# Twelve late attention slots as 64 tokens of two batches, in quarters and eighths of TensorE's array

## The chip, the cores and the metric

One core of a Trainium2 chip runs the kernel. The metric is device time in microseconds (us) of one execution; lower is better. TensorE (PE) multiplies, VectorE (DVE), ScalarE (ACT) and GpSimd (POOL) do elementwise work, SyncE (SP) issues most transfers. PEld is TensorE's loading of weights, which runs beside its matmuls. PSUM, which takes the results of matmuls, has 8 banks of 512 fp32 values for each of 128 partitions.

## The reference

A linear attention with a decaying state, whose output goes through a layer with a cosine gate. Only the shapes and the formulas that matter:

```
r, k, v: (4 batches, 8 heads, 768 tokens, 48), w, u: (8 heads, 48), fp32
for t in range(S):
    cur = einsum('bhd,bhe->bhde', u * k[t], v[t])
    y[t] = einsum('bhd,bhde->bhe', r[t], state + cur)
    state = w * state + einsum('bhd,bhe->bhde', k[t], v[t])
x = y.transpose(0, 2, 1, 3).reshape(3072, 384)
h = x @ w_in            # (384, 2048), float64 weights
out = (h * cos(h)) @ w_out   # (2048, 384), float64 weights; out is (3072, 384)
```

## The kernel before, in words

**Attention.** The recurrence is done in chunks of 128 tokens. There are 24 slots, one for each chunk of each batch (6 chunks, 4 batches): slot i is batch i % 4, chunk i // 4. In a slot, k and r are turned so that the head dimension lies on partitions (kT, rT: 4 pairs of heads, two heads on partitions 0 to 47 and 64 to 111) and scaled by powers of w (decT_k, decT_r). Then

- the scores: 8 matmuls, one a head, 48 rows by 128 columns, into two banks (mm_a, L819). The two heads of a pair lie in different row halves of the array;
- the diagonal with the bonus u (ACT, L809) and the mask, which copies the scores above the diagonal into it (DVE, L826): the result is A;
- x, the slot's output: a carried part from the state (mm_x, L840: 12 matmuls of 112 rows by 32 columns, four side by side in the array) and a direct part from A and v (mm_x2, L853: 16 matmuls of 128 rows by 32 columns), accumulated in one bank and split by ACT and DVE into two reduced-precision parts, xh and xl;
- the state of this batch: 8 matmuls of 128 rows by 48 columns (mm_z, L875), added to zc and decayed by DVE (L932, L933). The last chunk of a batch needs none.

All of these matmuls are fp32, and the profile shows two records for each.

**The layer.** Eight blocks of three slots (384 tokens). For each block and each of 16 slices f of the hidden dimension there is a step: nine matmuls into h (mm_h, L316), a chain of six operations between ACT and DVE for the gate (L327, L330, L333, L1030, L1033, L1036), and nine matmuls into the output (mm_o, L322). The first four blocks go through the slices in four pieces (UNITS), while the weights are being converted; the other four go through all 16 slices one after the other. Outputs of the first four blocks are added up in memory by transfers that POOL issues (L1078); those of the others are stored once, by SP (L1076), the very last by ACT (L1074).

**Late slots.** The first 12 slots (XS) run at the start. Slots 12 to 23 are late: each runs beside the steps of a block before its own, its matmuls set between those of the steps, in two groups: the scores, and later x with the state (mm_xz). Instead of transposing k and r with TensorE, SP loads them in rows of four tokens into a raw buffer (load_s, L693: four transfers a buffer, 32 partitions each), and DVE (L738) and POOL (L743) turn and scale them. The raw buffers (R_raw, two) are shared with the loads of the weights (L506, L511), which come a second time for a check of their range (L521, L532). PSUM banks 5 to 7 (B_ATT) serve the late slots.

**Order.** Every operation is an Op with an engine, a due time, an assumed cost, and what it comes after. A planner (Plan.order) lays them out by a greedy list, sixty times with changed due times, keeps the best by its own replay and fixes the order of each engine. The hardware then waits only where data or buffers ask for it.

Of the kernel before, what the change touches and what calls it, by code (L numbers as in the profile page):

```python
# [33 lines left out]
XS = 12  # L34
# [20 lines left out]
class Tile:  # L55
    def __init__(self, ap):
        self.ap, self.owner = ap, None

# [16 lines left out]
class Plan:  # L75
# [18 lines left out]
    @staticmethod  # L94
    def _free_at(tile):

        if tile.owner is None:
            return 0.0
        if any(o.end is None for o in tile.owner.users):
            return None  # L100
        return max(o.end + o.lat for o in tile.owner.users)

    def _ready(self, o):
        t = max((d.end + d.lat for d in o.after), default=0.0)
        picks, taken = [], set()
        for b in o.bufs:
            if b.tile is not None:
                continue
            best = None
            for tl in b.tiles:  # L110
                if id(tl) in taken:
# [6 lines left out]
            taken.add(id(best[1]))  # L118
            picks.append((b, best[1]))
            t = max(t, best[0])  # L120
        return t, picks

    def latest(self, order):
# [3 lines left out]
        for o in order:  # L127
# [8 lines left out]
            for b in o.bufs:  # L136
                owners = tiles.setdefault(b.tile, [])
                if not owners or owners[-1][0] is not b:
                    if all(b is not x for x, _ in owners):
                        owners.append((b, o))  # L140
# [10 lines left out]
    def replay(self, order, rng):  # L151

        free, port, prev, owner, end = {}, 0.0, {}, {}, {}
        for o in order:
            t = max((end[d] + d.lat for d in o.after), default=0.0)
            for b in o.bufs:
                if owner.get(b.tile) is not b:
                    prev[b] = owner.get(b.tile)
                    owner[b.tile] = b
                if prev.get(b) is not None:  # L160
                    t = max(t, max(end[d] + d.lat for d in prev[b].users))
# [35 lines left out]
    def one_pass(self):  # L197
        for o in self.ops:
            o.start = o.end = None
            for b in o.bufs:  # L200
                b.tile = None
                for tl in b.tiles:
                    tl.owner = None
# [13 lines left out]
        while len(done) < len(self.ops):  # L217
# [16 lines left out]
            for b, tl in picks:  # L234
                b.tile, tl.owner = tl, b
# [15 lines left out]
def kernel(  # L251
# [18 lines left out]
    C = 128  # L270
    NP = H // 2
# [5 lines left out]
    NJ = B * CPB  # L277
    TB = max(BLOCKS) * C
# [57 lines left out]
    with ExitStack() as actx:  # L336
# [3 lines left out]
        bank = [Tile(banks.tile([P, 512], F32, name=f"bank{i}")) for i in range(8)]  # L340
# [26 lines left out]

        zc = [att.tile([KP, NP, D], F32, name=f"zc{b}") for b in range(B)]
        R_zt = ring("zt", 2, [KP, NP, 2 * D], F32)
        wr = att.tile([NP, 2, DP], F32, name="wr")  # L370
# [8 lines left out]
        dec_k = att.tile([P, H, D], F32, name="dec_k")  # L379
        upper = att.tile([P, C], I32, name="upper")  # L380
        warm = att.tile([P, P], BF16, name="warm")
# [20 lines left out]
        def start_pool2():  # L402
            for t in R_zt:
                nc.gpsimd.memset(t.ap, 0.0)
# [11 lines left out]

        def start_dve():
# [5 lines left out]
        o_pool2 = op(POOL, -98, 3.0, start_pool2)  # L423
        o_dve = op(DVE, -99, 0.3, start_dve)
# [54 lines left out]
        o_dk = op(ACT, -6, 0.45, tab_copy, [o_tt], [b_tab])  # L479

# [175 lines left out]
        def chunk(i, due, xbuf):  # L656
            b, c = i % B, i // B
# [21 lines left out]
            late = i >= XS  # L679
            if late:  # L680
                rb = Buf(R_f)
                ks, rs = Buf(R_raw), Buf(R_raw)

            def rn():
                return heads(rb) if late else rb()[:, :, 0:D]
# [4 lines left out]
            def load_s(buf, src):  # L690
                def part(m, q, n_q, p, n_p, n):
                    j, d0 = m // 2, 32 * (m % 2)
                    nc.sync.dma_start(  # L693
                        staged(buf)[32 * m + q : 32 * m + q + n_q, p : p + n_p, 0:n],
                        bass.AP(
                            tensor=src.tensor,
                            offset=src.offset + ((b * H + 2 * p + j) * S + c * C + 4 * q) * D + d0,
                            ap=[[4 * D, n_q], [2 * S * D, n_p], [1, n]],
                        ),
                    )  # L700

                def go():
                    for m in range(3):
                        part(m, 0, 32, 0, NP, 4 * D)
                    if i < NJ - 1:
                        part(3, 0, 32, 0, NP, 4 * D)
                    else:

                        nc.gpsimd.memset(staged(buf)[96:P, NP - 1, 4 * D - 32 :], 0.0)
                        part(3, 0, 32, 0, NP - 1, 4 * D)  # L710
                        part(3, 0, 31, NP - 1, 1, 4 * D)
                        part(3, 31, 1, NP - 1, 1, 4 * D - 32)

                return go


            ahead = [last_A[0]] if late else []
            ln = "late" if late else None
            if late:
                l_ks = op(SP, due - 6.2, 2.2, load_s(ks, k), ahead, [ks], lat=4.0, line=ln)  # L720
                l_rs = op(SP, due - 6.1, 2.2, load_s(rs, r), ahead, [rs], lat=4.0, line=ln)
            l_k = op(SP, due - 5.2, 1.2, load(kb, k), ahead, [kb], lat=2.6, line=ln)
            l_r = op(SP, due - 5.1, 1.2, load_r, ahead, [rb], lat=2.6, line=ln)
            l_v = op(SP, due - 5.0, 1.2, load(vb, v), ahead, [vb], lat=2.6, line=ln)
# [9 lines left out]
            if late:  # L734
                def tr_s(dst, src):
                    def go():
                        blocks = staged(src).rearrange("q p (g x) -> q p g x", g=4)[:, :, :, 0:32]
                        nc.vector.transpose(dst().rearrange("q p (t g) -> q p g t", g=4), blocks)  # L738

                    return go  # L740

                def decay_s(dst, dec):
                    return lambda: nc.gpsimd.tensor_tensor(dst()[0:KP], dst()[0:KP], dec[0:KP], op=ALU.mult)  # L743

                t_k = op(DVE, due - 2.9, 0.95, tr_s(kT, ks), [l_ks], [ks, kT])
                e_k = op(POOL, due - 2.8, 1.4, decay_s(kT, decT_k), [t_k], [kT], port=True)
                t_r = op(DVE, due - 2.8, 0.95, tr_s(rT, rs), [l_rs], [rs, rT])
                e_r = op(POOL, due - 2.7, 1.4, decay_s(rT, decT_r), [t_r], [rT], port=True)
            else:
                t_r = op(PE, due - 2.4, 0.49, tr(rTp, rb), [l_r, o_pool], [rb, rTp, rT], lat=0.3)  # L750
                e_r = op(
                    DVE,
                    due - 2.2,
                    0.62,
                    lambda: nc.vector.tensor_tensor(rT()[0:KP], cube(rTp)[0:KP], decT_r[0:KP], op=ALU.mult),
                    [t_r, o_dtr],
                    [rTp, rT],
                )
# [29 lines left out]
            if not first and not late:  # L788
# [32 lines left out]
            last_A[0] = o_A = op(PE, due - 1.7, 1.25 if late else 1.1, mm_a, [e_k, e_r], [kT, rT, *Ap], lat=0.3)  # L821
# [426 lines left out]
```

## Time and profile before

| what | value |
|---|---|
| three runs, median | 513.16 us (512.38 to 513.32) |
| profiled execution, time | 512.26 us |
| profiled execution, span (first to last instruction) | 510.5 us |
| granted TensorE clock, mean | 0.999 |
| TensorE busy | 501.5 us, 98% of the span |
| DVE, ACT, POOL busy | 381.0, 331.0, 177.1 us |

Rows of groups read: line, engine, operation, output<-inputs, shapes, count | busy us, mean ns of one | idle time before and who ended it. A row of the chain has a start, a length, and the work. A row of waits has who waited for whom: us in total, times, the longest. A row of a timeline has start, length, engine, line and operation.

### The profile page before, as it was taken

The page shows a single profiled execution, that of the slowest core. Times are in us where ns is not written, and L with a number is a line of the kernel's source. Part 1 is how long each engine was busy: PE and PEld are TensorE (multiplying, and loading weights), DVE is VectorE, ACT ScalarE, POOL GpSimd, SP SyncE. Part 2 cuts the span into 40 slices and gives each one's busy share as a digit, 9 for nine tenths or more (in the row PEclk, how much of TensorE's full clock was granted, in tenths as well). Part 3 has the DMA queues.
Part 4 walks back from the last instruction along what each step waited for, and adds up shares of the span by engine and source line. Part 5 has one row for each costly group of instructions (what it writes and reads, how often), then busy time and mean ns, then how long its engine had stood idle before and what let it go on. Part 6 is the DMA issues. An engine that isn't in the chain of part 4 may idle for free.

```text
span 510.5 us, 11742 instructions
## 1 busy us (share of the span) xinstructions
PE 501.5 (98%) x4389; PEld 480.0 (94%) x4389; DVE 381.0 (75%) x773; ACT 331.0 (65%) x833; POOL 177.1 (35%) x184
## 2 busy tenths in 40 slices
PE   8999999999999999999999999999999999999995
PEld 5788899999999999999999999999999999999995
DVE  6898999888888875576777777777777767756553
ACT  2989987767667756556657465575665765655453
POOL 6777422445454451242426224224044041300000
PEclk9999999999999999999999999999999999999999
DMA  8999226586666593524676736446455465200001
GB/s 137 179 179 190 79 86 218 152 167 156 157 140 131 127 180 44 76 65 67 160 146 151 159 99 167 111 156 152 105 130 140 142 170 114 89 16 33 1 1 49
DMA packets 114975, 61.56 MB, mean 121 GB/s; under 512 B 78433, under 2 KB 110818, under 8 KB 114914
## 3 DMA queue, kind: packets, MB, share of 16 engines
q1 hardware_dynamic: 109586, 53.50, 42.7%
q0 software_dynamic: 5184, 7.08, 9.9%
q8 instruction: 35, 0.57, 0.5%
q14 instruction: 26, 0.21, 0.2%
q10 hardware_dynamic: 144, 0.20, 0.1%
HBM read 48.96 MB, written 11.80 MB: 119 GB/s over the span
## 4 chain that ended last, share of the span: by engine, by line
PE 94%; DMA 2%; DVE 1%; ACT 1%; issue 1%; POOL 0%; SPq 0%; DVEq 0%; POOLq 0%; ACTq 0%
PE bank L322 41%; PE bank L316 39%; PE bank L819 4%; PE bank L853 4%; PE bank L840 3%; PE bank L875 2%; PE bank L730 1%; DMA v<-in_v_dram 1%; DMA k<-in_k_dram 1%; ACT A L809 1%; PE bank L1094 0%; DVE pq L440 0%; POOL f L765 0%; DVE a L800 0%; DVE rq L447 0%
## 5 line engine op out<-in xcount | busy, mean ns | idle before, releaser
L322 PE MATMUL bank<-w_out_hi,gh 128*128 128x384 f32 x384 | 131.9, 344 | 0.0
L322 PE MATMUL bank<-w_out_hi,gl 128*128 128x384 f32 x384 | 129.8, 338 | 0.0
L316 PE MATMUL bank<-xh,w_in_lo 128*128 128x384 f32 x384 | 129.7, 338 | 0.0
L322 PE MATMUL bank<-w_out_lo,gh 128*128 128x384 f32 x384 | 129.5, 337 | 0.0
L316 PE MATMUL bank<-xh,w_in_hi 128*128 128x384 f32 x384 | 129.1, 336 | 0.0
L316 PE MATMUL bank<-xl,w_in_hi 128*128 128x384 f32 x384 | 128.8, 335 | 0.0
L330 DVE SCALAR_TENSOR_TENSOR f<-bank,qi 128x384 f32<-128x384 f32 (+1 forms) x132 | 71.4, 543 | 47.0 <-ACT qi L327 46.5
L327 ACT ACTIVATE qi<-bank 128x384 int32<-128x384 f32 (+1 forms) x132 | 62.8, 479 | 57.7 <-PE bank L316 57.0
L1033 ACT CAST gh<-f 128x384 fp32r<-128x384 f32 (+1 forms) x132 | 65.7, 500 | 48.9 <-DVE f L1030 46.9
L1030 DVE TENSOR_TENSOR f<-bank,f 128x384 f32<-128x384 f32 (+1 forms) x132 | 71.2, 542 | 32.5 <-ACT f L333 30.3
L1036 DVE TENSOR_TENSOR gl<-f,gh 128x384 fp32r<-128x384 f32 (+1 forms) x132 | 80.7, 613 | 19.6 <-ACT gh L1033 19.1
L333 ACT ACTIVATE f<-f 128x384 f32<-128x384 f32 (+1 forms) x132 | 67.3, 513 | 41.6 <-DVE f L330 40.8
L322 PEld LDWEIGHTS bank<-w_out_hi,gh 128*128 128x128 f32 x384 | 72.0, 188 | 3.0 <-issue 0.8
L316 PEld LDWEIGHTS bank<-xh,w_in_lo 128*128 128x128 f32 x384 | 72.2, 188 | 0.3 <-DVE w_in_lo L631 0.3
L316 PEld LDWEIGHTS bank<-xh,w_in_hi 128*128 128x128 f32 x384 | 72.2, 188 | 0.3 <-issue 0.2
L316 PEld LDWEIGHTS bank<-xl,w_in_hi 128*128 128x128 f32 x384 | 72.1, 188 | 0.0
L322 PEld LDWEIGHTS bank<-w_out_hi,gl 128*128 128x128 f32 x384 | 72.1, 188 | 0.0
L322 PEld LDWEIGHTS bank<-w_out_lo,gh 128*128 128x128 f32 x384 | 72.0, 188 | 0.0
L809 ACT ACTIVATE A<-ident,a 128x128 f32<-128x128 f32 x192 | 59.6, 391 | 4.9 <-DVE a L800 4.8
L743 POOL TENSOR_TENSOR kT<-kT,decT_k 112x512 f32<-112x512 f32 x12 | 15.6, 1301 | 129.3 <-DVE kT L738 74.4
L621 POOL TENSOR_TENSOR f<-f,raw 128x384 int32<-128x384 int32 x32 | 36.7, 1148 | 60.8 <-DVE f L610 31.7
L1078 POOL DMA_DIRECT2D out_dram<-f x36 | 32.7, 1012 | 40.6 <-DVE f L1030 17.2
(88 smaller groups left out, 589.5 us busy)
## 6 DMA issues: line engine op xcount, KB each, us to landing
raw<-in_moe_w_in_dram SPq DMA_DIRECT2D x32, 384.0 KB, 3.2
raw<-in_moe_w_out_dram SPq DMA_DIRECT2D x32, 384.0 KB, 3.2
out_dram<-f POOLq DMA_DIRECT2D x36, 192.0 KB, 4.5
k<-in_k_dram SPq DMA_DIRECT2D x24, 192.0 KB, 4.2
v<-in_v_dram SPq DMA_DIRECT2D x24, 192.0 KB, 5.1
raw<-in_k_dram SPq DMA_DIRECT2D x47, 96.0 KB, 3.1
raw<-in_r_dram SPq DMA_DIRECT2D x47, 96.0 KB, 2.1
out_dram<-f SPq DMA_DIRECT2D x23, 192.0 KB, 1.9
```

What stands on the lines that cost most here:

```text
L316: nc.tensor.matmul(ph, a, b_, start=(i == 0), stop=(i == len(mm) - 1))
L322: nc.tensor.matmul(acc, a[:, ts], b_[:, f, :], start=(first and i == 0), stop=(last and i == 2))
L327: nc.scalar.activation(qi, ph, AF.Copy, scale=INV_2PI, bias=0.25)
L330: nc.vector.scalar_tensor_tensor(q, ph, INV_2PI, qi, op0=ALU.mult, op1=ALU.subtract)
L333: nc.scalar.activation(q, q, AF.Sin, scale=TWO_PI, bias=0.5 * math.pi)
L621: lambda: nc.gpsimd.tensor_tensor(ai(), ai(), cn(), op=ALU.add),
L809: nc.scalar.activation(A[j]()[:, p, :], ident, AF.Copy, scale=ab()[:, h : h + 1])
L819: nc.tensor.matmul(cube(Ap[j])[:, p, :], kT()[ps, p, :], rT()[ps, p, :], start=True, stop=True)
L1030: nc.vector.tensor_tensor(g()[:, cs], ph()[:, cs], q()[:, cs], op=ALU.mult)
L1033: nc.scalar.copy(gh()[:, cs], g()[:, cs])
L1036: nc.vector.tensor_tensor(gl()[:, cs], g()[:, cs], f32(gh())[:, cs], op=ALU.subtract)
L1078: nc.gpsimd.dma_start(dst, ob(), accum_op=ALU.add)
```

## The change

The 12 late slots cut the last three chunks of each batch differently. A late slot now takes 64 tokens of two batches: slot i has the batches 2m and 2m + 1 with m = (i - 12) % 2, and the tokens from 384 + 64 * ((i - 12) // 2). On 128 partitions, 0 to 63 are the first batch and 64 to 127 the second.

- Scores: 16 matmuls of 48 rows by 64 columns, 64 moving columns; a head's row half and a batch's column half give a quarter of the array.
- State: 16 matmuls of 64 rows by 64 columns, in the same group as the scores (mm_az) and in the same pair of banks; in ten slots.
- x (mm_xx): the carried part is 24 matmuls of 112 rows by 32 columns with 64 moving columns; the direct part 32 matmuls of 64 rows by 32 columns, an eighth of the array each, written out in an order by hand.
- Two banks at a time are taken as a pair (P_ATT: banks 5 and 6, or 6 and 7); the planner's tiles have parts for that.
- A second decay table for 64 tokens (late_table) takes the place of the first in dec_k, once all early slots have used it, and ident2 and upper2 are made for the two halves.
- Loads: load_s issues eight transfers of 16 partitions a buffer; k, r and v come in two transfers of 64 rows each. Stores of late slots are two transfers of 64 rows; of the very last, the first half is issued by ACT and the second by SP.
- zc and zt hold two batches together; wr lies in the memory of dec_k.

```
+        bank_all = banks.tile([P, 8, 512], F32, name="bank")
+        bank = [Tile(bank_all[:, i]) for i in range(8)]
+        P_ATT = [Tile(bank_all[:, i : i + 2], bank[i : i + 2]) for i in (5, 6)]
...
+            def tab_t2():
+                pt = b_tab2().rearrange("q (p t) -> q p t", p=NP)
+                for p in range(NP):
+                    for b in range(2):
+                        nc.tensor.matmul(pt[b * CT : (b + 1) * CT, p, :], decT_k[:, p, mid], ident, start=True, stop=True)
...
+                def go():
+                    for n in range(4):
+                        for b in range(2):
+                            if i < NJ - 1 or n < 3 or b == 0:
+                                part(n, b, 0, 16, 0, NP, 4 * D)
...
+            l_ks = op(SP, due - 6.2, 3.9, load_s(ks, k), ahead, [ks], lat=3.0, line="late")
+            l_rs = op(SP, due - 6.1, 3.9, load_s(rs, r), ahead, [rs], lat=3.0, line="late")
+            l_k = op(SP, due - 5.2, 1.3, load(kb, k), ahead, [kb], lat=2.6, line="late")
...
+            def mm_az():
+                for p in range(NP):
+                    for j in range(2):
+                        ps = slice(j * DP, j * DP + D)
+                        for b in range(2):
+                            nc.tensor.matmul(
+                                score(j)[half[b], p, :],
+                                kT()[ps, p, half[b]],
+                                rT()[ps, p, half[b]],
+                                start=True,
+                                stop=True,
+                            )
+                if not more:
+                    return
+                z = z_of()
+                for p in range(NP):
+                    for j in range(2):
+                        for b in range(2):
+                            nc.tensor.matmul(
+                                z[j * DP : j * DP + DP, b, p, :],
+                                kb()[half[b], 2 * p + j, :],
+                                vb()[half[b], 2 * p + j, 0:D],
+                                start=True,
+                                stop=True,
+                            )
...
+            def mm_xx():
+                x = xp()[:, :, 0 : NK * CT].rearrange("q b (kk t) -> q b kk t", kk=NK)
+                for kk in range(NK):
+                    for b in range(2):
+                        for g in range(4 * kk, 4 * kk + 4):
+                            p, s = divmod(g, 3)
+                            gs = slice(G * (g % 4), G * (g % 4) + G)
+                            nc.tensor.matmul(
+                                x[gs, b, kk, :],
+                                zb()[:, b, p, G * s : G * s + G],
+                                rT()[0:KP, p, half[b]],
...
+                rounds = (
+                    ((0, 0), (1, 0), (2, 0), (3, 0)),
+                    ((4, 0), (1, 1), (6, 0), (7, 0)),
+                    ((4, 1), (5, 0), (10, 0), (7, 1)),
+                    ((8, 0), (9, 0), (10, 1), (11, 0)),
                 )
+                for group in rounds:
+                    for b in range(2):
+                        for g, n in group:
...
+                            nc.tensor.matmul(
+                                x[gs, b, g // 4, :],
+                                vb().rearrange("q h d -> q (h d)")[half[b], p * 2 * DP + at : p * 2 * DP + at + G],
+                                A[j]()[half[b], p, 0:CT],
...
                     def st(ob=ob, dst=dst, f0=f0, last=last):
+                        for n, (rows, to) in enumerate(dst):
+                            if last and n == 0:
+                                nc.scalar.dma_start(to, ob()[rows])
+                            elif f0 == 0:
+                                nc.sync.dma_start(to, ob()[rows])
+                            else:
+                                nc.gpsimd.dma_start(to, ob()[rows], accum_op=ALU.add)
```

More of the change, by code (lines that the diff above doesn't have):

```diff
@@ L136, in latest @@
             for b in o.bufs:
[L137 to L140, printed above, removed]
+                for part in b.tile.parts:
+                    owners = tiles.setdefault(part, [])
+                    if not owners or owners[-1][0] is not b:
+                        if all(b is not x for x, _ in owners):
+                            owners.append((b, o))
         for owners in tiles.values():
@@ L415, in start_pool2, with start_late @@
             )
+        def start_late():
+            nc.gpsimd.tensor_tensor(ident2, ident[:, 0:CT], ident[:, CT:C], op=ALU.add)
+            nc.gpsimd.tensor_copy(upper2[0:CT], upper[0:CT, 0:CT])
+            nc.gpsimd.tensor_copy(upper2[CT:P], upper[CT:P, CT:C])
         def start_dve():
@@ L674, in load @@
                 )
[L679 to L682, printed above, removed]
             def rn():
-                return heads(rb) if late else rb()[:, :, 0:D]
+                return rb()[:, :, 0:D]
             def load_r():
                 nc.sync.dma_start(rn(), r[b, :, c * C : (c + 1) * C, :].rearrange("h t d -> t h d"))
[L690 to L724, printed above, removed]
+            l_k = op(SP, due - 5.2, 1.2, load(kb, k), [], [kb], lat=2.6)
+            l_r = op(SP, due - 5.1, 1.2, load_r, [], [rb], lat=2.6)
+            l_v = op(SP, due - 5.0, 1.2, load(vb, v), [], [vb], lat=2.6)
             def tr(dst, src):
@@ L732, in tr @@
                 return go
[L734 to L758, printed above, removed]
+            t_r = op(PE, due - 2.4, 0.49, tr(rTp, rb), [l_r, o_pool], [rb, rTp, rT], lat=0.3)
+            e_r = op(
+                DVE,
+                due - 2.2,
+                0.62,
+                lambda: nc.vector.tensor_tensor(rT()[0:KP], cube(rTp)[0:KP], decT_r[0:KP], op=ALU.mult),
+                [t_r, o_dtr],
+                [rTp, rT],
+            )
             e0, c0, n0 = on(0)
@@ L787, in chunk @@
                 o_kd = op(e2, due - 2.7, c2, decay_k, [o_m, o_dk], [kb], port=True)
-            if not first and not late:
+            early_kd.append(o_kd)
+            if not first:
                 t_k = op(PE, due - 2.5, 0.49, tr(kTp, kb), [o_kd, o_pool], [kb, kTp, kT], lat=0.3)
@@ L935, in chunk @@
[L935 to L939 removed]
+                    w_c = pq[0:KP, None, :, 15:16].to_broadcast([KP, 2, NP, D])
+                    nc.vector.tensor_tensor(zc[m], z_of()[0:KP], zc[m], op=ALU.add)
+                    nc.vector.tensor_tensor(zc[m], zc[m], w_c, op=ALU.mult)
@@ new lines, in late_chunk, with xv, xo_ @@
+            xo = op(PE, due - 0.7, 1.8, mm_xx, [e_r, l_v, *e_A, *o_zt], [rT, xp, vb, zb, *A], lat=0.3)
+            def xv():
+                return xp()[:, :, 0 : NK * CT].rearrange("q b (kk t) -> q kk b t", kk=NK)
+            def xo_(n):
+                return xbuf()[n].rearrange("q kk (b t) -> q kk b t", b=2)
+            x_h = op(ACT, due - 0.4, 0.47, lambda: nc.scalar.copy(xo_(0), xv()), [xo], [xp, xbuf])
+            x_l = op(
+                DVE,
+                due - 0.2,
+                0.55,
+                lambda: nc.vector.tensor_tensor(xo_(1), xv(), f32(xo_(0)), op=ALU.subtract),
+                [x_h],
+                [xp, xbuf],
+            )
```

275 lines of the change are left out of this document (204 added, 71 removed).

## The prediction

> **What bounds the kernel now.** I first read the shares on the page, then the waits of TensorE, then the chain of the work that ended last around single slots. The shares and the waits:
>
> ```profile
> span 510.5 us, 11742 instructions
> PE 501.5 (98%) x4389; PEld 480.0 (94%) x4389; DVE 381.0 (75%) x773; ACT 331.0 (65%) x833; POOL 177.1 (35%) x184
> PE 94%; DMA 2%; DVE 1%; ACT 1%; issue 1%; POOL 0%; SPq 0%; DVEq 0%; POOLq 0%; ACTq 0%
> PE bank L1094 <- DVE pq L419: 1.2, 1, 1.2
> PE bank L853 <- DVE A L826: 0.8, 1, 0.8
> PE bank L472 <- DVE decT_k L456: 0.7, 1, 0.7
> ```
>
> TensorE is busy 98% of the span and 94% of the chain is its matmuls. What it waits for is small and belongs to the start: the largest wait is 1.2 us, under the warm-up matmuls. So whatever TensorE time a slot of the attention gives back or takes, the end moves by the same amount, as long as no new wait appears. The chain around the first late slot, and two others, with the whole length of the two steps into which the slot's matmuls are inserted:
>
> ```profile
> 212.12 1.05 PE bank L322 x6
> 213.17 1.09 PE bank L819 x16
> 214.26 0.72 PE bank L322 x3
> ...
> 217.61 0.79 PE bank L840 x24
> 218.40 0.90 PE bank L853 x32
> 219.30 0.49 PE bank L875 x16
> ...
> 58.91 1.99 PE bank L819 x32
> 60.89 0.85 PE bank L875 x32
> 222.09:223.67 1.58, 1.58 (x10) 1.00 0.11 26
> 212.12:214.99 2.87, 2.87 (x27) 1.00 0.83 123
> 216.55:220.52 3.97, 3.97 (x83) 1.00 0.11 22
> 444.01:447.47 3.46, 3.46 (x66) 1.00 0.02 5
> ```
>
> The columns of the last four rows are the stretch, its length, TensorE's busy time, its granted clock (1.00), DMA share and GB/s. Nine output matmuls (L322) alone take 1.58 us. With the scores (L819) among them the stretch is 2.87, so scores cost 1.29. With x (L840, L853) and state (L875) it is 3.97, so they cost 2.39; without state, in one of the last four slots, 3.46, so 1.88. **A late slot costs 3.68 us with state and 3.17 without; 8 and 4 of them make 42.1 us.**
>
> These costs split into rounds and a fixed part. An fp32 matmul leaves two records. Scores come two at a time (two row halves, 128 columns): sixteen records more (x32 against x16) add 1.99 - 1.09 = 0.90 us, 0.1125 per pair. State, also in pairs but 48 columns wide, adds 0.85 - 0.49 = 0.36, 0.045 per pair. Both are near a straight line in the moving columns; at 64 columns it gives **0.0585 us a round**. x comes four at a time: 24 and 32 records are 6 and 8 rounds, and 0.90/8 = 0.1125 again. The fixed part (entering and leaving a group of small matmuls) is then 1.29 - 8 x 0.1125 = 0.39 for scores, 1.88 - 14 x 0.1125 = 0.30 for x, and 0.51 - 8 x 0.045 = 0.15 for the state behind x.
>
> **The change part by part.** *Scores and state, one group (mm_az).* 16 score matmuls of 64 rows by 64 columns are 32 records; four fit in the array at once, so 8 rounds x 0.0585 = 0.47 (now 0.90). State is 16 matmuls, 32 records, 8 rounds, of the same shape, so no fixed part between. Its moving side stays 48 columns (0.045 a round, 0.36), but its weights grow from 48 to 64 columns, which may set the pace at 0.0585; I take that, 0.47 (now 0.36). With 0.39 fixed: **1.33, or 0.86 in the two slots without state.** State is now needed in ten slots, not eight.
>
> *x (mm_xx).* The carried part keeps 112 rows, so only four fit: 48 records, 12 rounds, 0.70 (now 0.68). The direct part has 64 rows by 32 columns, eight at once: 64 records, 8 rounds, 0.47 (now 0.90). Fixed: 0.30, and 0.15 for the change of shape between the two (the value of the state's, the only change of shape inside a group that the trace has). **1.62.**
>
> Sum: 10 x 2.95 + 2 x 2.48 = 34.5, against 42.1: **-7.6 us**. The unshown step is that quarters and eighths really overlap and that records are started fast enough, below.
>
> *The second decay table (late_table).* Eight plain matmuls, K 128 by 64 columns, two at once: 16 records, 8 rounds x 0.1125 + 0.39 = 1.3 us, once, in the saturated stretch. If each leaves one record, as the transposes of the first table do, 0.84. I take **+1.3**. Its copy on ACT (0.5) hides under the matmuls.
>
> *Stores.* Each late slot's store is two issues on SP, and the very last is half on ACT and half on SP, behind the four halves of the two slots before it.
>
> ```profile
> 504.70 0.94 SPq L1076 DMA_DIRECT2D out_dram<-f  x2
> 505.76 0.38 ACTq L1074 DMA_DIRECT2D out_dram<-f  x1
> out_dram<-f ACTq DMA_DIRECT2D x1, 192.0 KB, 3.0
> 240.22 1.74 SPq L693 DMA_DIRECT2D raw<-in_r_dram  x4
> 253.61 1.76 SPq L693 DMA_DIRECT2D raw<-in_k_dram  x4
> 244.42 1.29 POOL L743 TENSOR_TENSOR kT<-kT,decT_k 112x512 f32<-112x512 f32 x1 [9.73 <-DVE kT L738]
> 250.25 1.34 POOL L773 TENSOR_TENSOR k<-k,dec_k 128x384 f32<-128x384 f32 x1
> 258.23 1.09 PE bank L819 x16
> L809 ACT ACTIVATE A<-ident,a 128x128 f32<-128x128 f32 x88 | 27.4, 390 | 1.3 <-DVE a L800 1.3
> L826 DVE COPY_PREDICATED A<-upper,bank 128x512 f32<-128x512 int32 x24 | 16.3, 734 | 2.1 <-PE bank L819 2.0
> L933 DVE TENSOR_TENSOR zc<-zc,pq 112x192 f32<-112x192 f32 x8 | 2.9, 358 | 0.3
> SPq L693 <- ACT f L521: 64.5, 18, 14.1
> ```
>
> Five halves at 0.47 from 504.70 put the last issue at 506.58, 0.82 later than now; it carries half the bytes of a transfer that lands 3.0 us after its issue. The end moves between -0.2 (landing time cut by a third) and +0.8 (not cut). **+0.3.**
>
> *Loads on SP.* The staged loads go from 4 to 8 issues a buffer and the others from 1 to 2: 11 become 22 a slot. At 1.75/4 = 0.44 that is 9.7 us of SP instead of 4.8, per slot of about 22 (scores at 213.17, then 258.23 two slots on). Queued behind them on SP are the check loads of the weights, the next slot's loads and the stores; the 64.5 us row shows SP waiting for the shared raw buffers. What hides it: the k of the slot whose scores start at 258.23 was decayed by 251.6, kT by 245.7. So 6.6 us are spare, above the 4.9 added even if none of it ran ahead. Cost 0; with the cover gone, up to what the scores are late.
>
> *ACT, DVE, POOL.* The diagonals (eight of 0.39 a slot) and the mask (0.73) halve in columns, the state adds a second batch to 0.36 twice; together they shrink. All run beside TensorE: 0. The pair of banks that scores and state share must be free before x of the same slot; in this slot order 4.4 us lie between them (213.17 to 217.61), against two masks (now 2 x 0.73, halved) and a state of some 1.1 (an estimate: 0.36 twice, on twice the columns). 0.
>
> *The order.* The planner searches again with other costs, and the start up to about 64 us, where all waits stand, will be ordered differently. No row prices this; all of TensorE's idle time is 510.5 - 501.5 = 9 us, so +-1.5, centre 0.
>
> **Sum:** -7.6 + 1.3 + 0.3 = -6.0. The profiled execution took 512.26 (span 510.5), giving 506.3. It stands 0.9 under the median of the three runs, 513.16; against that, **507.2**. Own range, 505 to 509.5.
>
> **The rivals.** *One: TensorE cannot start small matmuls that fast.* The plan has 10 x 176 + 2 x 144 = 2048 records, mostly 7 to 15 ns apart; the densest sustained pace shown is the state's 0.36 us/16 = 22.5 ns. Windows of 30 ns inside x show its start:
>
> ```profile
> 217.60:217.63 0.03, 0.03 (x4) 0.03 (x8) 1.00 0.00 0
> 217.71:217.74 0.03, 0.03 (x8) 0.03 (x4) 1.00 0.00 0
> ```
>
> Four matmuls run at 217.60; at 217.71 four more have joined within 30 ns, so a burst starts at under 10 ns each. That speaks against the rival, but the pauses between bursts (0.11 us) may be what lets the queue refill. At 22.5 ns each: 2048 x 0.0225 + 10.1 fixed (12 x 0.84) = 56.2, +14.1, with table and stores +15.7: **528.9**. It decides from (42.1 - 1.6 - 10.1)/2048 = 14.8 ns a record on: above that the change loses. Chance 0.22: slower 0.16, no change 0.03, a small gain 0.03. The Trainium skill has rules on both sides, in TensorE: Matmul & The Clock Gate. Its section "Wait — 56ns, not 53.3ns?" says starts never come closer than about 25 ns however few the columns; as a floor for all records that would make 2048 x 0.025 + 10.1 + 1.6 = 62.9 against 42.1, an estimate of 534. Its section "Measured speedup vs the span model" has packed tiles starting about 4 ns apart and sixteen tiles giving 10.6 times. The trace agrees with the second for bursts of four, and shows nothing as dense as this plan for long.
>
> *Two: quarters do not overlap four at a time, only in pairs.* The trace has row halves (scores) and column quarters (x), never both at once. Then a slot has 60 rounds with state (16 + 16 + 12 + 16) and 44 without: 10 x (0.84 + 3.51) + 2 x (0.84 + 2.57) = 50.3, +8.2, and 1.6: **523.0**. Against it: each kind overlaps fully where it appears, at the same 0.1125. Chance 0.08.
>
> *Three: supply.* Doubled issues make scores wait; half a us a slot leaves 6.0 - 6.0 = 0, **513.2**. For it: SP's 64.5 us row; against: the 6.6 us spare. Chance 0.07 (no change 0.03, small gain 0.03, slower 0.01).
>
> **How the numbers follow.** The forecast has 0.63, the rivals 0.22, 0.08 and 0.07. Three runs spread by 0.94 us, so 0.2% is about what can be told from no change. Faster: 0.63 + 0.03 + 0.03, and 0.01 for small gains in rival two, 0.70; no change 0.06; slower 0.24. The range starts at 504.0 (every table, store and order term at its good end) and goes up to 514.5, which takes in rival three and rival one up to about 15.5 ns a record; the rest, some 2 in 10, lies above.
>
> **What would show it.** Right: the step with scores and state is about 2.9 us long (1.58 + 1.33) and with x 3.2; score and state records come in fours 0.058 us apart, the direct part of x in eights; TensorE's waits stay at the start; the table's matmuls take about 1.3. Rival one: evenly spaced starts of 15 ns or more. Rival two: pairs 0.058 apart. Rival three: waits of the scores on kT, rT or k. The prediction is wrong above all if small matmuls start more slowly than 14.8 ns apiece.

## The result, and the profile after

The changed kernel takes **516.18 us** (median of 8 runs, 514.12 to 517.85) against 512.59 for the kernel before beside it (8 runs, 511.86 to 513.32): ratio **1.0069 [1.0049, 1.0088]**. It is 0.7% slower; 507.2 was forecast and 514.5 was the end of the range. The profiled execution took 515.86 with a span of 514.1, that of before 512.26 with 510.5: +3.6 in time, and +3.5 in the span when it is not rounded. The page and the waits of TensorE after the change:

```profile
span 514.1 us, 14178 instructions
PE 500.0 (97%) x5464; PEld 476.3 (93%) x5464; DVE 384.7 (75%) x777; ACT 332.3 (65%) x834; POOL 175.6 (34%) x186
PE 78%; DMA 6%; DVE 4%; ACT 4%; issue 2%; SPq 2%; POOL 1%; DVEq 0%; ACTq 0%; POOLq 0%
PE bank L815 <- ACT kT L786: 1.9, 2, 1.2
PE bank L331 <- DVE f L1240: 1.9, 2, 1.3
PE bank L1312 <- DVE pq L444: 1.2, 1, 1.2
PE bank L337 <- DVE f L1282: 0.6, 1, 0.6
PE bank L1040 <- POOL rT L987: 0.4, 1, 0.4
PE bank L1053 <- POOL k L1005: 0.3, 1, 0.3
PE bank L337 <- DVE gl L1246: 0.2, 1, 0.2
```

TensorE is busy 1.5 us less (501.5 to 500.0), in a span that is 3.5 longer. Its own share of the chain fell from 94% to 78%; transfers and SP, 2% and 0% before, hold 6% and 2%. New among the waits are five that belong to the steps and the late slots: h waits for the gate's f (L331), the output for the copy that empties its bank (f, L1282) and for gl (L337), scores for rT, state for k.

Where in the span? I timed the start of every step by its first matmul into h. Step 20 is past the crowded start, step 124 is near the end. A stall is two records of TensorE that start more than 0.3 us apart, from step 20 on, less the usual 0.18; "out" is from the start of the last matmul to the end of the span.

| profiled execution | step 20 starts | steps 20 to 124 | stalls in them | out |
|---|---|---|---|---|
| before | 119.34 | 368.91 | 0 | 5.67 |
| after | 122.45 | 368.31 | 4.7 in 8 | 6.71 |
| after - before | +3.1 | -0.6 | +4.7 | +1.0 |

So there are three losses, start, stalls and stores, and one gain, inside the -0.6. The gain shows in the chain and the stretches around the first late slots (stretch, length, busy time of PE, PEld, DVE, ACT and POOL, clock, DMA share, GB/s):

```profile
216.28 0.62 PE bank L1040 x32
...
220.69 0.81 PE bank L1102 x48
...
215.23:218.08 2.85, 2.85 (x74) 2.54 (x74) 2.06 (x5) 1.53 (x4) 0.04 (x1) 1.00 0.92 137
219.64:223.01 3.37, 3.37 (x123) 2.93 (x122) 1.38 (x4) 1.67 (x4) 0.00 (x0) 1.00 0.18 38
423.32:427.27 3.95, 3.95 (x52) 3.63 (x51) 2.88 (x7) 2.40 (x7) 2.56 (x3) 1.00 0.78 230
212.09:213.67 1.58, 1.58 (x10) 1.58 (x10) 1.40 (x3) 0.97 (x2) 0.35 (x2) 1.00 0.61 76
```

The bare step of nine output matmuls still takes 1.58. With scores and state it is 2.85, so they cost 1.27 (forecast 1.33); with x 3.37, so 1.79 (1.62); the third stretch is a whole step (1.56 + 1.58 bare) with scores alone, 0.81 (0.86). Ten slots of 3.06 and two of 2.60 are 35.8 us against 42.1: -6.3. In the trace the records of the scores, the state and the carried part start in fours, four within 20 ns, and the rounds follow some 0.058, 0.058 and 0.056 us apart. The direct part starts in eights only for its first half; its 64 records start within 0.64 us, where eight rounds of 0.0585 would have been 0.47. That is where x is longer than forecast.

### The profile page after: what moved, and what is told of

Same layout as the page of the kernel before. It is cut to its first block, busy times and chain, and to the rows that moved or that the text cites. A ratio compares the mean times of both kernels' runs of the same rounds, so it can differ in the third digit from the quotient of the medians.

```text
span 514.1 us, 14178 instructions
## 1 busy us (share of the span) xinstructions
PE 500.0 (97%) x5464; PEld 476.3 (93%) x5464; DVE 384.7 (75%) x777; ACT 332.3 (65%) x834; POOL 175.6 (34%) x186
## 3 DMA queue, kind: packets, MB, share of 16 engines
q0 software_dynamic: 5184, 7.08, 10.0%
## 4 chain that ended last, share of the span: by engine, by line
PE 78%; DMA 6%; DVE 4%; ACT 4%; issue 2%; SPq 2%; POOL 1%; DVEq 0%; ACTq 0%; POOLq 0%
PE bank L337 34%; PE bank L331 33%; PE bank L815 2%; DMA raw<-in_r_dram 1%; PE bank L1102 1%; PE bank L1124 1%; SPq L944 1%; ACT A L805 1%; PE bank L741 1%; PE bank L849 1%; DMA f<-in_r_dram 1%; DMA v<-in_v_dram 1%; DVE f L345 1%; PE bank L1040 1%; PE bank L836 1%
## 5 line engine op out<-in xcount | busy, mean ns | idle before, releaser
L337 PE MATMUL bank<-w_out_hi,gh 128*128 128x384 f32 x384 | 132.0, 344 | 0.6 <-DVE f L1282 0.6
L331 PE MATMUL bank<-xh,w_in_hi 128*128 128x384 f32 x384 | 129.8, 338 | 1.9 <-DVE f L1240 1.9
L337 PE MATMUL bank<-w_out_hi,gl 128*128 128x384 f32 x384 | 130.0, 338 | 0.2 <-DVE gl L1246 0.2
L331 PE MATMUL bank<-xh,w_in_lo 128*128 128x384 f32 x384 | 129.5, 337 | 0.0
L337 PE MATMUL bank<-w_out_lo,gh 128*128 128x384 f32 x384 | 129.4, 337 | 0.0
L331 PE MATMUL bank<-xl,w_in_hi 128*128 128x384 f32 x384 | 128.7, 335 | 0.0
L1246 DVE TENSOR_TENSOR gl<-f,gh 128x384 fp32r<-128x384 f32 (+1 forms) x132 | 81.8, 621 | 22.6 <-ACT gh L1243 22.1
L1240 DVE TENSOR_TENSOR f<-bank,f 128x384 f32<-128x384 f32 (+1 forms) x132 | 70.9, 540 | 28.4 <-ACT f L348 26.5
L331 PEld LDWEIGHTS bank<-xh,w_in_hi 128*128 128x128 f32 x384 | 72.1, 188 | 3.5 <-DVE f L1240 2.9
L337 PEld LDWEIGHTS bank<-w_out_hi,gh 128*128 128x128 f32 x384 | 72.0, 187 | 3.3 <-DVE f L1282 0.9
L337 PEld LDWEIGHTS bank<-w_out_hi,gl 128*128 128x128 f32 x384 | 72.0, 188 | 0.9 <-DVE gl L1246 0.9
L331 PEld LDWEIGHTS bank<-xh,w_in_lo 128*128 128x128 f32 x384 | 72.1, 188 | 0.0
L331 PEld LDWEIGHTS bank<-xl,w_in_hi 128*128 128x128 f32 x384 | 72.1, 188 | 0.0
L337 PEld LDWEIGHTS bank<-w_out_lo,gh 128*128 128x128 f32 x384 | 72.0, 188 | 0.0
L667 POOL TENSOR_TENSOR f<-f,raw 128x384 int32<-128x384 int32 x32 | 34.8, 1087 | 62.0 <-DVE f L656 43.7
L805 ACT ACTIVATE A<-ident,a 128x128 f32<-128x128 f32 x96 | 30.2, 392 | 3.4 <-DVE a L796 3.4
```

Source lines behind the costliest of these rows:

```text
L331: nc.tensor.matmul(ph, a, b_, start=(i == 0), stop=(i == len(mm) - 1))
L337: nc.tensor.matmul(acc, a[:, ts], b_[:, f, :], start=(first and i == 0), stop=(last and i == 2))
L667: lambda: nc.gpsimd.tensor_tensor(ai(), ai(), cn(), op=ALU.add),
L805: nc.scalar.activation(A[j]()[:, p, :], ident, AF.Copy, scale=ab()[:, h : h + 1])
L1240: nc.vector.tensor_tensor(g()[:, cs], ph()[:, cs], q()[:, cs], op=ALU.mult)
L1246: nc.vector.tensor_tensor(gl()[:, cs], g()[:, cs], f32(gh())[:, cs], op=ALU.subtract)
```

## The experiments

The stalls had two theories at first. **S**: SP's time. Twenty-two issues a slot instead of eleven make loads late. **R**: the raw buffers. Eight issues hold a raw buffer longer than four, and the loads of the weights' check use the same two buffers. This is SP's timeline around the stall at 303 us (start, length, line, count):

```profile
284.41 4.64 SPq L944 DMA_DIRECT2D raw<-in_k_dram  x8
289.15 4.74 SPq L944 DMA_DIRECT2D raw<-in_r_dram  x8
294.00 1.30 SPq L934 DMA_DIRECT2D k<-in_k_dram  x2
295.40 1.27 SPq L934 DMA_DIRECT2D f<-in_r_dram  x2
296.77 0.57 SPq L552 DMA_DIRECT2D raw<-in_moe_w_in_dram  x1
297.43 1.28 SPq L934 DMA_DIRECT2D v<-in_v_dram  x2
...
SPq L944 <- ACT f L567: 21.5, 8, 8.4
```

Eight issues take 3.6 to 5.6 us in this trace, here 4.7, against 1.74 for four in the prediction's rows. In the last slot a buffer takes ten issues, not eight. The last row, of SP's waits in the late stretch (from 205 us on), says that eight staged loads waited, 21.5 us in all and up to 8.4, until ACT (L567, the check) had read a raw buffer. Everything else for the slot stands behind them on SP. The chain of this stall goes on from there:

```profile
295.40 0.59 SPq L934
296.05 3.23 DMA f<-in_r_dram
299.44 1.02 POOL f L999
300.46 1.56 POOL rT L987
302.01 0.98 POOL k L1005
303.04 0.78 PE bank L1053 x32
```

r is issued at 295.40 and the chain has its transfer until 299.28; POOL, in order, then does f, rT and k, and only then can the state run.

The largest late wait, h for the gate's f (L331), has a chain too. The first row is SP's timeline for the last slot, the next three are the chain, and the last three are waits of DVE, ACT and POOL in the late stretch:

```profile
433.01 6.51 SPq L944 DMA_DIRECT2D raw<-in_r_dram  x10
438.88 2.27 DMA raw<-in_r_dram
441.37 1.08 DVE rT L980
442.45 0.40 DVE f L1240
...
DVE rT L980 <- DMA raw<-in_r_dram: 5.0, 3, 3.3
ACT f L567 <- DMA v<-in_v_dram: 5.3, 4, 1.7
POOL f L999 <- DMA f<-in_r_dram: 17.5, 8, 5.0
```

The staged r lands at 441.15. DVE stands for it 3.28 us, turns it, and only then does the gate's f that h waits for, at 442.89. So a late load reaches TensorE through engines that work in order. In all DVE waits 9.3 us for staged loads and ACT's check (L567) 10.1 us for loads, where before neither has such a wait and POOL's is 4.2. One of the eight stalls is none of this: the 0.8 us at 259.7 stands behind a long gl of DVE (last section).

**e1, whole transfers.** Each raw buffer in four transfers of 32 partitions, k, r and v in one. It loads 128 tokens of one batch instead of 64 of two, so the late slots compute with other tokens.

```
-                    for b in range(2):
-                        nc.sync.dma_start(dst()[half[b], :, 0:D], src[2 * m + b, ...])
+                    nc.sync.dma_start(dst()[:, :, 0:D], src[2 * m, :, tw : tw + C, :]...)
...
+                        part(n, 0, 0, 32, 0, NP, 4 * D)
```

> The changed kernel, with the late loads issued as before: 4 transfers of 32 partitions a raw buffer and one each for k, r and v (11 a slot, not 22), for the same bytes. To have that, each late slot loads 128 tokens of one batch, not 64 of two, so its second batch's rows are other tokens (that part of the result is left out). Order, matmuls, stores and all else as in the changed kernel. Theory S (the second issues: SP has 22 of about 0.55 us a slot, loads come late, the late slots' matmuls and the gate chain behind them wait): the stalls of some 5 us in the late stretch go, the first matmul of step 124 comes 5 to 6 us earlier than in the changed kernel, time about 511 against 516.2, so 1 to 2 us under the kernel before. Rival R (the raw buffers shared with the check loads are what is short): 1 to 2 us come back. Rival O (the order written by the planner is bad by itself, whatever the loads): no change, 516.

Measured: 511.17 us, 0.9976 [0.9961, 0.9992]. Steps 20 to 124 take 363.03, stalls 0.3. The order of TensorE's work is that of after, so nearly all of the stall comes from the split loads, and 363.03 - 368.91 = -5.9 is what the quarters and eighths bring when fed.

**e2, no check.** Loads as in the change, but the check of the weights' range loads and computes nothing.

```
-            o0 = op(SP, due - 3.0, 1.6, lambda: load_raw(i, raw), [behind], [raw], lat=3.4)
+            o0 = op(SP, due - 3.0, 1.6, lambda: None, [behind], [raw], lat=3.4)
```

> The changed kernel without the second reading of the weights: the 32 check loads and their two operations on ACT and DVE are left out (the flag is then set from constants); order and all else the same. Theory S: SP loses about 2.7 issues a slot out of 25 (some 0.5 us each), so most stalls stay: 514 to 516. Rival R: the raw buffers are free for the staged loads, stalls go: about 511. Rival O: 516.

Measured: 511.28 us, 0.9974 [0.9957, 0.9991]; steps 20 to 124 in 363.12, no stall. TensorE's largest wait in it:

```profile
PE bank L806 <- ACT kT L777: 1.9, 2, 1.2
```

It stands in the start; the L331 wait (L1240's f) is gone, as in e1. In the same order, twenty-two issues a slot do no harm when the check is out of the way.

**e3, only the loads split.** The kernel before, with its late slots' loads in twice as many transfers.

```
+                    if n_q == 32:
+                        part(m, 0, 16, p, n_p, n)
+                        part(m, 16, 16, p, n_p, n)
+                        return
```

> The kernel before with one part of the change alone: its late loads issued in twice as many transfers of half the rows (8 a raw buffer, 2 each for k, r and v). Same bytes, same order, same matmuls. Theory S: stalls appear in the late stretch of a kernel that had none; its slots have some 0.6 us more TensorE time to hide them, so +2 to +5 us (515 to 517.5). Rivals R and O: no change within 0.5 us, 512.6.

Measured: 522.39 us, 1.0177 [1.0143, 1.0210]; steps 20 to 124 in 379.29, +10.4, with 8.7 of stalls. The split alone costs more than the whole change. The expectation for R was worked out wrongly here: it forecast no change, though the split lengthens the hold of the raw buffers in this kernel too. So e3 does not tell S from R; e9 and e12 were made for that. TensorE's and SP's largest wait in e3 (SP's from 210 us on):

```profile
PE bank L322 <- ACT f L1078: 1.8, 3, 1.3
...
SPq L708 <- ACT f L521: 32.7, 13, 10.6
```

**e4, another order.** The planner's search starts from another random number: `random.Random(10)` instead of 9.

> The changed kernel with another seed of the planner's search (10, not 9), so another order of the start; nothing else is edited. By the planner's own sums this order has step 20 2.5 us earlier. If the 3.1 us that the changed kernel is behind at step 20 are the order's, step 20 comes at 120 us (122.45 in the changed kernel, 119.34 before) and the time is 1 to 3 us less, 513 to 515; if they are a cost of the change itself (the second table, its place in the start), step 20 stays within 1 us of 122.45. The late stretch gets another order too, whose stalls this does not foretell.

Measured: 513.89 us, 1.0014 [0.9995, 1.0032]. Step 20 at 120.74 (-1.7), stalls 4.0. Another order helps the start, and leaves the stalls nearly whole.

**e5, a third raw buffer.** It lies in the memory of the r ring, and the staged loads and the check take turns in three.

```
+        R_raw3 = R_raw + [Tile(raw3, R_r)]
-            ks, rs = Buf(R_raw), Buf(R_raw)
+            ks, rs = Buf(R_raw3), Buf(R_raw3)
```

> The changed kernel with a third raw buffer for the staged loads of late slots and the check loads; it lies in the memory of the two r buffers of the early slots, which late slots do not use. SP still has 22 issues a slot. The planner writes another order with it (one late slot's matmuls move ahead of step 48), so the stretch to compare is step 20 to step 124: 368.3 us in the changed kernel, 368.9 before, 363.0 with 11 issues a slot or without check loads. Theory R (raw buffers are short): 363 to 364. Theory S (SP's issue time by itself is too long for a slot): 366 or more. The start is ordered anew as well, so the whole time may lie between 511 and 516.

Measured: 516.04 us, 1.0061 [1.0033, 1.0088], no faster in all. Steps 20 to 124 take 365.14, 3.2 less than after, and step 20 comes at 124.83, 2.4 later. But the planner made another order, and in the trace the first late slot's scores and state run at 104.5 us, ahead of step 20. With their 1.27 put back the stretch is 366.4 (an estimate), only 1.9 less than after. The stalls are 2.2 instead of 4.7, 1.3 of them from 210 us on. So e5 lies between the two theories' forecasts as it was measured, and at S's when the work is made equal: the smaller stalls speak for the buffers, but e5 does not decide.

**e6, k, r and v issued by ACT.** `nc.scalar.dma_start` in load().

> The changed kernel with the six issues a slot for k, r and v of the late slots given by ACT, not SP; they stand at the same place of the written order. SP keeps 16 staged issues a slot and the check loads; the raw buffers are held as before. Theory S: SP is free sooner, most of the 5 us of stalls go, step 48 to 124 takes 275 to 277 us (280.4 in the changed kernel), time 511 to 513. Theory R: the raw buffers are as short as they were, 279 to 281, time 515 to 517. A rival to both: ACT, which runs in order, is held by its own issues (6 x 0.4 us a slot, or waits for buffers) and the gate chain with it: 281 or more, 517 or more.

Measured: 535.31 us, 1.0439 [1.0390, 1.0487]; stalls 18.8. ACT in order is the gate's engine too, and here is what it did (timeline, then ACT's wait):

```profile
363.48 1.29 ACTq L934 DMA_DIRECT2D v<-in_v_dram  x2
366.66 0.53 ACT L348 ACTIVATE f<-f 128x384 f32<-128x384 f32 x1 [2.71 <-DMA v<-in_v_dram]
ACT f L348 <- DMA v<-in_v_dram: 5.7, 2, 3.0
```

The gate's activation idles 2.71 us, and the trace puts that down to v's transfer. The edit takes SP's load away, but puts its own cost in the place, so it says nothing between S and R.

**e7, the last store by ACT alone.** `if last:` for `if last and n == 0:`.

> The changed kernel with both halves of the very last store issued by ACT (the second half was on SP, ahead of the two halves of the slot before). Nothing else is edited. From the last matmul to the end of the span it is 6.7 us in the changed kernel and 5.6 before. If the queue of five issues on SP is the cause, this falls to 5.5 to 6.0 and the time by about 1 us, to 515.2; if the landing of half transfers is, it stays at 6.5 or more.

Measured: 517.85 us, 1.0074 [1.0050, 1.0098]. The forecast of 515.2 was missed. The way out is 6.28 instead of 6.71, between the two expectations and still 0.6 over before. Steps 20 to 124 took 371.03 with 7.0 of stalls in the same order of matmuls: the same order stalls differently from run to run, which fits that the runs of after spread by 3.7 us and those of before by 1.5.

**e8, the table by transfers.** The second decay table is two transfers of rows of dec_k and a copy, with no matmul and no bank.

```
-                        nc.tensor.matmul(pt[b * CT : (b + 1) * CT, p, :], decT_k[:, p, mid], ident, ...)
+                    nc.sync.dma_start(b_tab2()[b * CT : (b + 1) * CT], dec_k...[rows])
...
-            o_t2 = op(PE, 110, 0.5, tab_t2, [o_tt], [b_tab2], lat=0.3)
+            o_t2 = op(SP, 20, 1.2, tab_t2, [o_dk, *early_kd], [b_tab2], lat=2.6)
```

> The changed kernel with its second decay table made without TensorE and without a PSUM bank: rows 32 to 95 of the first table are copied to both halves of a buffer by two transfers, after the early slots, and from there into dec_k by ACT. In the changed kernel the table's matmuls ran at 9.3 us and their bank was held until the copy at 59.7 us, so the early slots had six banks, not seven. The planner orders the start anew. Theory B (that bank): step 20 at 120 to 120.8 (122.45 in the changed kernel, 119.34 before), time 1.5 to 2.5 us less, 513.5 to 515. Rival (the order of the start by chance, or the 1.0 us of matmuls alone): 121.4 to 122.5.

Measured: 514.92 us, 1.0032 [1.0016, 1.0049]. Step 20 at 120.91 (-1.5), just outside theory B's range and not in the rival's; steps 20 to 124 as in after (368.05, stalls 4.4). Rows of the table in the trace of after, its chain piece and the two operations (count, duration min/median/max in ns, first and last start):

```profile
9.27 1.02 PE bank L518 x16
L518 PE MATMUL bank<-ident,decT_k x16: 272/273/323, 9.2 to 10.0; 128*64 128x128 f32 x16
L522 ACT COPY dec_k<-bank x1: 477/477/477, 59.7 to 59.7; 128x384 f32<-128x384 f32 x1
```

The matmuls take 1.02 us at 9.3 us, but the copy that frees their bank runs at 59.7, after the last early slot has read the first table. For 50 us one of the seven banks that the early slots have is out of use. That this delays the start is not shown: e4 holds the bank nearly as long (its copy runs at 56.7 us), has the table's matmuls too, and comes to step 20 at 120.74, no later than e8. The planner ordered the start anew in both.

**e9, only k, r and v split.** The kernel before, raw loads whole, the other three transfers in halves: 14 issues a slot instead of 11.

> The kernel before with only k, r and v of its late slots issued in two halves of 64 rows: 3 issues more a slot; the staged loads stay at 4 a raw buffer, so the raw buffers are held as before. With all loads split (e3) step 48 to 124 went from 281.0 to 291.4 us. Theory S (SP's issue time): 3 of the 11 added issues, so 2 to 4 us of the 10.4 come back, 283 to 285, time 515 to 517. Theory R (what hurts is how long the staged loads hold the two raw buffers, which the check loads share): 281 to 282, time within 0.8 us of the kernel before.

Measured: 513.63 us, 0.9998 [0.9980, 1.0016]; steps 20 to 124 in 368.91, to the hundredth as before, no stall. SP's wait in the late stretch:

```profile
SPq L704 <- ACT f L521: 51.6, 16, 14.1
```

SP still has 51.6 us of this wait (64.5 before, 32.7 in e3): the added issues eat waiting time and nobody else's.

**e12, e3 without the check.** All 22 issues a slot, as many for a raw buffer as in e3, but no check loads, ACT reads or DVE operations.

> The kernel before with all late loads split as in e3 (22 issues a slot) and the check loads with their operations on ACT and DVE left out. With the split alone, step 48 to 124 was 291.4 us against 281.0. Theory R (raw buffers held longer by eight issues, shared with the check loads): with nobody to share them the 10.4 us go, 281 to 282, and the time is within 1 us of the kernel before. Theory S (22 issues by themselves keep SP too long): 286 or more, 517 or more.

Measured: 512.59 us, 0.9998 [0.9987, 1.0009]; 368.91, no stall. With e3, in the same order of matmuls, this settles S as it was put: the same 22 issues cost 10.4 us with the check and nothing without. The issues alone do no harm; the split loads and the check together do. e2 and e12 take away all of the check at once: its use of the raw buffers, its place in SP's queue, and ACT's and DVE's work, with ACT's waits for its loads. Which of them carries most of the 5 us is not shown, and e5 does not decide it.

**e10, three repairs.** e8 and e7, start_late after the early slots, and the checks spread out: every third step from 55 on, where the late slots load, and every step from 106 on, where they no longer do. The read of the check's flag moves eight steps back with them.

```
-        look = {lo + (NS - 16 - lo) * i // (2 * NF): i for i in range(2 * NF)}
+        for i in range(2 * NF):
+            look[55 + 3 * i if i < 17 else 106 + i - 17] = i
```

> The changed kernel with three edits, one for each place where it lost time. The second table by two transfers from the first (as in e8), and the small tables ident2 and upper2 made after the early slots: step 20 at 118.5 to 120 us (122.45). The check loads every third step while late slots run (17 of them) and every step from 106 on (15): step 48 to 124 in 275.5 to 278 us (280.4 in the changed kernel, 281.0 before). Both halves of the last store by ACT: 6.3 us from the last matmul to the end (6.7). In all about 509, 0.6 to 1% under the kernel before. If the stalls of the late slots do not come from sharing SP and the raw buffers with the check loads, the late stretch stays at 279 or more and the time at 512 to 513. Danger: the checks now crowd the last steps, whose DVE work they share; then the stretch from step 112 on grows by 1 us or more.

Measured: **509.03 us, 0.9907 [0.9885, 0.9928]**, faster than both kernels. Its page, TensorE's largest wait, and SP's for the check in the late stretch:

```profile
span 507.2 us, 14138 instructions
PE 497.2 (98%) x5448; PEld 476.3 (94%) x5448; DVE 376.8 (74%) x777; ACT 333.2 (66%) x834; POOL 178.0 (35%) x186
PE bank L1313 <- DVE pq L444: 1.2, 1, 1.2
SPq L944 <- ACT f L567: 27.5, 11, 9.1
```

There is no stall from step 20 on. Step 20 comes at 120.17 (+0.8 over before, just over its range), steps 20 to 124 take 363.20 (-5.7), out is 7.08 (+1.4, where 6.3 was expected), and with 0.1 between step 124 and the last matmul the span is -3.4. All checks are done; only their places differ. SP's staged loads still wait 27.5 us for the check's reader, more than the 21.5 of after, so such a wait is not a stall by itself. And the planner made another order here as well.

**e11, true costs.** e10, but the planner is told what SP's issues take: 4.6 for a raw buffer, 1.4 for k, r and v, 0.55 for a check's load (3.9, 1.3 and 1.6 before).

> As e10, and the planner told what the profile shows for SP: 4.6 us for the eight issues of a raw buffer (3.9 assumed in the change), 1.4 for two halves (1.3), 0.55 for a check load (1.6). Its own sum is 3 us longer than with the costs of the change, because it then sees waits on TensorE that it could not see. If the stalls come from an order written for shorter loads, the chip follows this plan more closely and the time is like e10 or up to 1 us less; if capacity (SP and raw buffers) is what is short, knowing it does not help: 0 to 3 us more than e10.

Measured: 513.19 us, 0.9993 [0.9981, 1.0006]; steps 20 to 124 in 367.43, stalls 3.9. This is 4.2 us more than e10, outside both forecasts. The checks stand at the same steps as in e10, so the thinner checks do not remove the stalls by themselves: in this order 3.9 of them are left. e10's gain is that of thinner checks and of its order together, and no run here tells them apart.

## Why the prediction was wrong, step by step

| term | forecast | measured | from |
|---|---|---|---|
| late slots on TensorE | -7.6 | -5.9 | e1, e2 against before, steps 20 to 124 |
| loads on SP | 0 | +5.3 | 368.31 - 363.03 |
| table and order | +1.3 and 0 | +3.1 | step 20 |
| stores | +0.3 | +1.0 | out |
| sum | -6.0 | +3.5 | span +3.5 |

**The late slots: right in mechanism.** Quarters overlap four at a time at the forecast pace, and records follow each other fast enough. Rivals one (14.8 ns a record as the turning point) and two (pairs only) fall: a whole group has 10 to 15 ns between records, and the price came out as a gain. Of the 7.6, 1.7 are missing. By single stretches the slots come to -6.3: x costs 1.79 instead of 1.62, 2.0 us over twelve slots, and scores with state cost 0.7 less than forecast. The missing part of x is the direct part, whose eighths took 0.64 us and not the 0.47 of the sum. The other 0.4, between these few slots and the whole stretch, is not traced. On the rule of the Trainium skill (TensorE: Matmul & The Clock Gate, "Wait — 56ns, not 53.3ns?") that starts never come closer than about 25 ns, the trace disagrees for tiles side by side: the four records of a round start 7 ns apart, and the 48 of the carried part 14 ns apart on average.

**"Loads on SP ... Cost 0": the step that failed.** It read 6.6 us spare from one slot and set them against 4.9 us of added SP time, and so put the doubled loads at nothing. The runs show +5.3 in steps 20 to 124 (e1 and e2 against after). The comparison fails in two ways. The added time was too small: the 22 issues of a slot took 12 to 13.5 us in after, not 9.7, and the 11 of the slot read there 5.3, so some 7 to 8 us were added, more than the 6.6. And SP's time does not decide it, for e2 and e12 have the 22 issues and no stall. What the sum left out is the check that shares SP and the two raw buffers: a buffer's issues went from 1.74 us to 3.6 to 5.6. The prediction quoted the 64.5 us row, saw in it that SP waits for these buffers, and gave it to rival three, but put no price on a longer hold. Rival three was right in kind, with 0.07 of the chances and priced at half a us a slot in delay; 5.3 us over twelve slots is 0.44.

That it takes both is shown, in two orders: e1 and e2 against after (-5.3 and -5.2), and e3 with e12 (+10.4 with checks, 0 without). How late loads become stalls is shown by the chains above: DVE, ACT and POOL work in order, stand for a load, and the gate stands behind them. "ACT, DVE, POOL ... 0" in the prediction counted their work and not this. How much of it is the hold of the buffers, and how much SP's order or ACT's wait for the check's loads, stays open: e5 (a third buffer), e10 and e11 (thinner checks, no stall in one order and 3.9 in another) each changed the order with it.

**"The order ... centre 0": failed too.** Step 20 was +3.1 late. The table's 1.02 us is close to the forecast 1.3, but it fell in the start and not in the saturated stretch, and its bank was held for 50 us, which the prediction did not price. e8, without matmuls and bank, takes 1.5 off; another order with both of them (e4) takes 1.7 off, and e10 2.3. Part of it is noise: the order of before puts step 20 between 119.22 (e12) and 120.81 (e9). So an order as good as e8's exists with the bank held, and the cause of what is left of the +3.1 stays open; so does start_late's part, which ran only together with others in e10.

**Stores: mis-sized.** +0.3 was the middle between a half that lands a third sooner (-0.2) and one that does not (+0.8). The rows of after (issues, then size and median us to landing):

```profile
507.20 3.33 SPq L1294 DMA_DIRECT2D out_dram<-f  x5
508.26 0.57 ACTq L1292 DMA_DIRECT2D out_dram<-f  x1
out_dram<-f SPq DMA_DIRECT2D x23, 96.0 KB, 2.5
out_dram<-f ACTq DMA_DIRECT2D x1, 96.0 KB, 2.7
```

A half takes 3.33/5 = 0.67 us to issue, the waits between included (0.47 was assumed, from the whole transfers), and lands hardly sooner: ACT's in 2.7 us against 3.0 for the whole one before, SP's in 2.5. The pessimistic end of that step, +0.8, was nearer. With the stores of after, out lies between 6.71 and 7.42 in seven runs (after, e1, e2, e4, e5, e6, e8); with both last halves on ACT it is 6.28 in e7, 6.91 in e11 and 7.08 in e10; with the stores of before 5.67 to 6.06. So e7's 0.4 is no more than the spread, and who issues the last half does not settle it.

## What to carry to other kernels

Before a transfer is cut in two at no cost, find the buffer that it fills, who else takes turns in it, and which engines stand in order behind a load that comes late: here the 22 issues cost nothing alone and 5 to 10 us beside another user of the same queue and buffers. A long wait of a queue for a buffer's reader says that the buffer is contended, and no more: 64.5 us before and 27.5 in e10 went without a stall, 32.7 in e3 with 8.7 of them. And when an edit makes a planner write another order, a difference of a few us belongs to the edit and the order together, until a run in the old order parts them.

## What the runs showed of the hardware

*A VectorE operation beside GpSimd took five times as long.* Timeline of after, DVE's gl twice, and POOL's operations beside the second:

```profile
253.88 0.55 DVE L1246 TENSOR_TENSOR gl<-f,gh 128x384 fp32r<-128x384 f32 x1
256.25 2.90 DVE L1246 TENSOR_TENSOR gl<-f,gh 128x384 fp32r<-128x384 f32 x1
...
256.46 1.30 POOL L1005 TENSOR_TENSOR k<-k,dec_k 128x384 f32<-128x384 f32 x1
257.45 1.28 POOL L1002 TENSOR_TENSOR f<-f,u_b 128x384 f32<-128x384 f32 x1
```

The same operation is 0.55 us alone and 2.90 beside two POOL operations. In this trace none of the 102 that run beside no elementwise operation of POOL takes over 0.56, and 11 of the 30 that do take over 1.1; it does not happen each time (0.55 at 302.9 beside 0.59 of POOL). Behind the 2.90 stands the stall at 259.7. The Trainium skill (GPSIMD Engine Reference, Specifications) says that the two engines share their way into SBUF and that VectorE's instructions with two SBUF inputs contend; gl has two inputs, and the trace agrees.

*The clock halved after a gap.* In e7 two matmuls started 2.43 us apart at 444 us; these are the stretch with it and the next (columns as above):

```profile
444.00:448.00 4.00, 1.91 (x9) 1.58 (x8) 2.03 (x4) 0.90 (x2) 1.28 (x1) 0.85 0.61 121
448.00:452.00 4.00, 4.00 (x46) 3.50 (x45) 1.79 (x5) 1.96 (x5) 2.68 (x3) 0.72 0.75 223
```

The granted clock, 1.00 before, falls to 0.85 and then, with TensorE busy all the time, 0.72. These are means: for 446.83 to 450.22 alone it is 0.50, and 1.00 after. At half the clock 3.4 us lose 1.7 (an estimate), so a stall can cost more than itself, and six of the 14 gaps counted as e7's stalls are plain matmuls 0.32 us apart in this stretch. In e3 the clock is 0.50 from 324.72 to 328.10, behind two matmuls 1.60 us apart, and ten of its 21 gaps stand there; 1.59 us at 443 in after and at 407 in e3 left it at 1.00. So the length of one gap does not tell.
